# Second layer of the last two chunks by seven block products: decay attention and softplus FFN on one Trainium2 core

## The chip, the cores and the metric

The kernel runs on one core of one Trainium2 chip. Times are device microseconds of one execution. An execution's own time is a little longer than the span between its first and last instruction, and both are given where it matters. Engines are named as in the profile: PE (matmul) and PEld (its weight loads), DVE (vector), ACT (scalar), POOL (GpSimd), SP (the engine that issues most DMAs).

## The reference

```python
for b in range(nb):                       # nb = 12 blocks of 64 tokens
    qb, kb, vb = (q[:, :, sl], k[:, :, sl], v[:, :, sl])
    intra = einsum(qb, kb) * Dmask        # Dmask[i, j] = lam ** (i - j) for i >= j, else 0
    out[:, :, sl] = intra @ vb + (qb * lam_pow) @ kv_state
    kv_state = lam ** 64 * kv_state + (kb * rev_pow).T @ vb
x = out.transpose(0, 2, 1, 3).reshape(B * S, H * D)       # (3072, 512)
h = x @ w_in                                              # w_in (512, 2048)
g = maximum(h, 0) + log1p(exp(-abs(h)))                   # softplus
y = g @ w_out                                             # w_out (2048, 512)
```

All arrays are float32; q, k, v are (4, 8, 768, 64): batch 4, 8 heads, 768 tokens, 64 features.

## The kernel before

The sequence is cut into six chunks of 128 tokens (`NCH = 6`); a chunk holds these tokens of all four batches, 512 columns. Per chunk there is the attention (pairs of heads, `NP = 4`, called units), then two layers. To keep float32 accuracy at the fast matmul type, each operand is held as a high and a low part, and each product is three matmuls: high by high, high by low, low by high. d_ff = 2048 is cut into `NF = 16` blocks f of 128.

- Chunks 0 and 1 (`STD = 2`) run both layers plainly: `mlp1` (L421) and `mlp2` (L442). In this stretch the weights are also converted, the attention of later units is run, and the weights' parts go to DRAM scratch: `g1`, `g2` (blocks of w_in with the sums of blocks that the seven products need, made by `block_sums` and `store_sums`, L518 to L532) and `g3` (w_out).
- Chunks 2 and 3, and chunks 4 and 5, are taken in pairs. Their first layer uses seven products of blocks in place of eight (Winograd's form of Strassen): a product is one pair of f blocks i, a pair of halves of d_model, a pair of chunks. `product` (L588) does one, six matmuls. In the loop over c = 2, 4 and i = 0 to 7 the order on PE is P1 (bank a), P6 (bank b), P5 (bank c), P2 (adds into a), P7 (into b), P4 (into b), P3 (into c). ACT copies P1 out of a to `p1` (L757) before P2 may add into a; DVE makes `u2` (L759) before P7 may add into b. What comes out is softplus of h for f blocks 2i and 2i+1 of chunk c, split into `ga` and `gb`, and of chunk c+1, kept in `lb`.
- The second layer is plain: `second` (L607), three matmuls for one f block and one batch b, accumulating over f in four banks. For chunk c its steps are put between the products of the next iteration (`rest`, run in shares of 2, 4 and 2); for chunk c+1 they follow as a block after the loop, with operands split as they go. `finish` copies a bank and sends the output.
- In the loop for c = 2 one attention unit per iteration is run as well: `k_decay` (ACT, L289) and `q_decay` (DVE, L296) at its start, `event` near its end. At its end stands `low_of(gb, c21)` (DVE, L599). At i = 1 of c = 2 the last block sums of w_in are made: `block_sums(7)`, `store_sums(7)`, `send_sums(7)`.

The order is written out by hand: every engine runs its instructions in program order, and waits where an operand or a buffer is not ready. Buffers come from pools by size: 21 of 8 KB a partition (`t8`), 7 of 4 KB (`t4`), 5 of 2 KB (`t2`); a load on SP waits until one is free. PSUM has four banks for outputs (`obank`), two for `bank`, and a double one for `work`.

Of the kernel before, what the change touches and what calls it, by code (L numbers as in the profile page):

```python
# [32 lines left out]
def decay_attention_softplus_ffn(  # L33
# [12 lines left out]
    dr = ctx.enter_context(tc.tile_pool(name="dr", bufs=1, space=bass.MemoryType.DRAM))  # L46
# [383 lines left out]
    def mlp2(ss):  # L430
        c = ss[0] // NF
        ends = ss[-1] % NF == NF - 1
        if ss[0] % NF == 0:
            o_tiles[c] = [obank(f"o{c}_{b}") for b in range(B)]
        if ends:
            ob = t8([128, B, 512], F32, f"ob{c}")
        for b in range(B):
            for s in ss:
                f = s % NF
                g, w = g_tiles[s], w_second(s)  # L440
                for n, (i, j) in enumerate(((0, 0), (0, 1), (1, 0))):
                    nc.tensor.matmul(  # L442
                        o_tiles[c][b], lhsT=g[:, i, b * 128 : (b + 1) * 128], rhs=w[:, j],
                        start=f == 0 and n == 0, stop=f == NF - 1 and n == 2,
                    )
            if ends:
                copy = nc.vector.tensor_copy if b % 2 else nc.scalar.copy
                copy(out=ob[:, b], in_=o_tiles[c][b])
                queue = nc.scalar if c == NCH - 1 and b % 2 == 0 else nc.sync
                queue.dma_start(out=out[b * S + c * C : b * S + (c + 1) * C, :], in_=ob[:, b])  # L450

    def w_group(j):
        return (2 * j, 2 * j + 1) if 2 * j < NW else ()
# [90 lines left out]
    def load_w1(i):  # L544
        a, b = t8([128, 2, 4, 256], F32R, f"w1a{i}"), t8([128, 2, 3, 256], F32R, f"w1b{i}")
        nc.sync.dma_start(out=a.bitcast(F32), in_=g1[i])
        nc.sync.dma_start(out=b.bitcast(F32), in_=g2[i])
        w1_tiles[i] = a, b
# [49 lines left out]
    def low_of(g, l):  # L598
        nc.vector.tensor_sub(out=g[:, 1], in0=l, in1=g[:, 0])  # L599
# [12 lines left out]
    def finish(c, b):  # L612
        if c not in obs:
            obs[c] = t8([128, B, 512], F32, f"ob{c}")
        end = c == NCH - 1 and b % 2
        copy = nc.vector.tensor_copy if end else nc.scalar.copy
        copy(out=obs[c][:, b], in_=outs[c, b])
        queue = nc.sync if end else nc.scalar
        queue.dma_start(out=out[b * S + c * C : b * S + (c + 1) * C, :], in_=obs[c][:, b])

    def seconds(c, fs, ends=False):

# [105 lines left out]
    run(old_seconds([last - 4, last - 3]))  # L728
    rest = old_seconds([last - 2, last - 1], True)
    nxt = 4 * NP + 1  # L730
    for c in range(STD, NCH, 2):
        more = c + 2 < NCH
        lb = {}
        gs = {}
        for i in range(NF // 2):
            if more and i == 1:
                block_sums(NF // 2 - 1)
                store_sums(NF // 2 - 1)
                send_sums(NF // 2 - 1)
            unit = nxt if more else None  # L740
            if unit is not None:
                load_upto(unit + 2)
            if i + 1 < NF // 2:
                load_w1(i + 1)
            load_w2(i)
            if unit is not None and unit < NG:
                k_decay(unit)
                q_decay(unit)
            if i % 2 == 0:
                l4 = t8([128, 4, 512], F32, f"lb{c}_{i}")  # L750
            for n in range(2):
                lb[2 * i + n] = l4[:, 2 * (i % 2) + n]
            ta, tb = t4([128, 2, 512], F32, f"ta{c}_{i}"), t4([128, 2, 512], F32, f"tb{c}_{i}")
            p1, u2, u3, c21 = ta[:, 0], ta[:, 1], tb[:, 0], tb[:, 1]
            a, b_ = bank(f"a{c}_{i}"), work(f"b{c}_{i}")[:, 0]
            product("P1", i, a)
            nc.scalar.copy(out=p1, in_=a)  # L757
# [12 lines left out]
            low_of(ga, la)  # L770
            run(rest, 2)
            product("P4", i, b_, False)
            nc.vector.tensor_add(out=c21, in0=b_, in1=p1)
            nc.scalar.activation(c21, c21, AF.Softplus)
            gb = parts_of(f"g{c}_{2 * i + 1}", c21)
            product("P3", i, c_, False)
            nc.vector.tensor_add(out=u2, in0=c_, in1=u2)
            nc.scalar.activation(lb[2 * i], u2, AF.Softplus)
            run(rest, 4)
            if unit is not None and unit <= NG:  # L780
                event(unit)
                nxt += 1
            low_of(gb, c21)
            run(rest)
            pair = [(2 * i + n, (ga, gb)[n], w2_tiles[i][:, n]) for n in range(2)]
            rest = seconds(c, pair, i == NF // 2 - 1)
        ahead = 2
        def split(f):
            gs[f] = parts_of(f"g{c + 1}_{f}", lb[f])
            low_of(gs[f], lb[f])  # L790
        for f in range(ahead):
            split(f)
        for i in range(2):
            load_w2(i)
        run(rest)
        xc.clear()
        steps = []
        if more:
            steps = [lambda n=n, m=m: x_block(n, xr[c + 2][:, m + (2 if n == "P2" else 0)], m) for n in ("P1", "P2") for m in range(2)]
            for n in range(2):  # L800
                steps += [lambda n=n: x_sums_early(c + 2, n), lambda n=n: x_sums_late(c + 2, n)]
        for f in range(NF - 2):
            if f % 2 == 0 and f // 2 + 2 < NF // 2:
                load_w2(f // 2 + 2)
            if f + ahead < NF:
# [7 lines left out]
    run(rest)  # L813


def _layout(q, k, v, lam, w_in, w_out):
# [37 lines left out]
```

## Time and profile before

| | |
|---|---|
| time, median of 3 runs | 597.03 us (596.62 to 598.16) |
| profiled execution: time, span | 595.9 us, 594.1 us |
| PE busy | 576.5 us, 97% of the span |
| DVE busy | 321.6 us, 54% |
| ACT busy | 256.8 us, 43% |
| HBM read, written | 112.20 MB, 29.36 MB |
| granted PE clock | 0.999 of full speed |

The profile gives busy time and idle time by engine, by line and by stretch of time; a wait is put down to the instruction that ended it. An average over the span hides that the stretches differ: the first 226 us hold the attention, the conversion of weights and the plain chunks, the rest the two pairs of chunks. A row of a timeline reads: start, duration, engine, line, operation, output and inputs, shapes, how many were merged, and in square brackets the idle time before it with what ended it.

### The profile page before, as it was taken

To read this page: it belongs to the slowest core of one execution; us is meant where nothing else is said; L and a number is where in the kernel's file an instruction comes from. 1 tells how busy PE (TensorE), PEld (TensorE's weight loads), DVE (VectorE), ACT (ScalarE), POOL (GpSimd) and SP (SyncE) were. 2 spreads that over 40 slices of the span, in tenths; PEclk is the share of its full clock that TensorE was granted. 3 is DMA by queue.
4 is the path that set the end of the run, shared out by engine and by line. 5 is a ranking of instruction groups with operands and counts; after the bars stand their busy time and mean duration, and the time that the engine had idled before them with its cause. 6 is when DMAs were issued, how large, how long until landed. Compare 5 with 4: busy or idle time off the path is not lost.

```text
span 594.1 us, 12014 instructions
## 1 busy us (share of the span) xinstructions
PE 576.5 (97%) x5203; PEld 469.4 (79%) x5203; DVE 321.6 (54%) x492; ACT 256.8 (43%) x416; POOL 4.1 (1%) x11
## 2 busy tenths in 40 slices
PE   8899989989999999989999999999999999999997
PEld 6677778768888888778888888888888888888886
DVE  7779998974767768664543443295133333333410
ACT  3777776663345434543333332463142222224310
POOL 2000000000000000000000000000000000000000
PEclk9999999999999999999999999999999999999999
DMA  8997565883999974649965647489267454473101
GB/s 292 407 407 272 186 202 178 273 298 114 327 399 387 412 285 172 253 159 386 413 257 188 237 171 271 155 315 375 88 237 294 167 190 140 137 288 121 56 1 71
DMA packets 38452, 142.34 MB, mean 240 GB/s; under 512 B 3712, under 2 KB 5760, under 8 KB 31360
## 3 DMA queue, kind: packets, MB, share of 16 engines
q1 hardware_dynamic: 35808, 136.86, 62.7%
q10 hardware_dynamic: 2592, 4.72, 2.1%
q8 instruction: 41, 0.67, 0.5%
q14 instruction: 11, 0.09, 0.0%
HBM read 112.20 MB, written 29.36 MB: 238 GB/s over the span
## 4 chain that ended last, share of the span: by engine, by line
PE 76%; DVE 10%; DMA 8%; ACT 2%; issue 1%; SPq 1%; DVEq 0%; ACTq 0%
PE o L607 30%; PE b L588 11%; PE h L421 8%; PE o L442 8%; PE c L588 7%; PE a L588 7%; DMA att<-in_att 4%; DMA g<-w 3%; PE x L311 2%; PE z L326 2%; DVE c L235 2%; DVE st L343 2%; DMA raw<-in_wts 1%; DVE w L242 1%; DVE c L229 1%
## 5 line engine op out<-in xcount | busy, mean ns | idle before, releaser
L607 PE MATMUL o<-w,g 128*128 128x512 f32 x816 | 192.7, 390 | 0.0
L607 PEld LDWEIGHTS o<-w,g 128*128 128x128 f32 x816 | 152.5, 188 | 31.9
L421 PE MATMUL h<-x,w 128*128 128x512 f32 x384 | 94.4, 395 | 2.1 <-DVE w L242 2.1
L421 PEld LDWEIGHTS h<-x,w 128*128 128x128 f32 x384 | 70.9, 188 | 19.9 <-DVE w L242 3.7
L442 PE MATMUL o<-w,g 128*128 128x512 f32 x336 | 82.3, 393 | 1.1 <-DVE w L242 0.8
L442 PEld LDWEIGHTS o<-w,g 128*128 128x128 f32 x336 | 62.3, 188 | 15.1 <-DVE w L242 1.2
L588 PE MATMUL a<-xcP,w1a 128*128 128x512 f32 x192 | 49.0, 391 | 1.5 <-ACT ta L757 1.5
L588 PE MATMUL b<-xcP,w1b 128*128 128x512 f32 x192 | 48.8, 389 | 0.0
L759 DVE TENSOR_TENSOR ta<-b,ta 128x512 f32<-128x512 f32 x16 | 11.0, 690 | 60.9 <-PE b L588 60.9
L588 PEld LDWEIGHTS a<-xcP,w1a 128*128 128x128 f32 x192 | 35.9, 188 | 9.8 <-ACT ta L757 2.3
L588 PEld LDWEIGHTS b<-xcP,w1b 128*128 128x128 f32 x192 | 36.0, 188 | 7.5
L402 ACT ACTIVATE l<-h 128x512 f32<-128x512 f32 x32 | 19.0, 595 | 49.1 <-PE h L421 46.5
L599 DVE TENSOR_TENSOR g<-lb,g 128x512 fp32r<-128x512 f32 x32 | 21.1, 688 | 34.1 <-ACT g L595 34.1
L767 DVE TENSOR_TENSOR tb<-b,ta 128x512 f32<-128x512 f32 x16 | 11.1, 691 | 50.4 <-PE b L588 50.4
L338 DVE TENSOR_TENSOR a<-x,mask 128x512 f32<-128x512 f32 x15 | 10.4, 691 | 44.1 <-PE y L313 23.4
L410 DVE TENSOR_TENSOR g<-l,g 128x512 fp32r<-128x512 f32 x32 | 22.1, 690 | 18.8 <-ACT g L406 18.7
L764 ACT ACTIVATE la<-a 128x512 f32<-128x512 f32 x16 | 9.6, 598 | 52.3 <-PE a L588 52.3
L757 ACT COPY ta<-a 128x512 f32<-128x512 f32 x16 | 9.3, 584 | 51.8 <-PE a L588 51.8
L595 ACT CAST g<-lb 128x512 fp32r<-128x512 f32 x32 | 18.7, 619 | 18.4 <-PE o L607 17.6
L588 PE MATMUL b<-xcP,w1a 128*128 128x512 f32 x96 | 24.9, 391 | 0.8 <-DVE xcP L561 0.4
L326 PEld LDWEIGHTS z<-qd,st 64*64 64x64 f32 x640 | 17.0, 134 | 10.0 <-issue 9.7
L386 ACT COPY xr<-z 128x512 f32<-128x512 f32 x16 | 9.4, 585 | 36.0 <-PE z L330 35.5
(100 smaller groups left out, 774.4 us busy)
## 6 DMA issues: line engine op xcount, KB each, us to landing
w<-g SPq DMA_DIRECT2D x39, 1024.0 KB, 5.6
att<-in_att SPq DMA_DIRECT2D x48, 512.0 KB, 10.0
raw<-in_wts SPq DMA_DIRECT2D x32, 512.0 KB, 10.2
w1a<-g SPq DMA_DIRECT2D x16, 1024.0 KB, 6.8
g<-w SPq DMA_DIRECT2D x24, 512.0 KB, 9.3
w1b<-g SPq DMA_DIRECT2D x16, 768.0 KB, 6.7
g<-parts SPq DMA_DIRECT2D x16, 512.0 KB, 9.0
out_dram<-ob ACTq DMA_DIRECT2D x18, 256.0 KB, 2.0
```

The source lines that it names most:

```text
L235: nc.vector.tensor_add(out=c, in0=c, in1=raw_at(ks, 0))
L311: nc.tensor.matmul(x[r, cols], lhsT=k[r, b, t], rhs=q[r, b, t], start=True, stop=True)
L326: nc.tensor.matmul(w[half(t), s, cols], lhsT=st[r, b, t], rhs=qd[r, b, t], start=True, stop=False)
L343: nc.vector.scalar_tensor_tensor(out=to[:, :, t], in0=of[:, :, t], scalar=lam_c[r, h : h + 1], in1=u[:, :, t], op0=ALU.mult, op1=ALU.add,)
L402: nc.scalar.activation(l_tiles[s], h_tiles.pop(s), AF.Softplus)
L410: nc.vector.tensor_sub(out=g[:, 1, :], in0=l_tiles.pop(s), in1=g[:, 0, :])
L421: nc.tensor.matmul(h_tiles[s], lhsT=w[:, i, cs], rhs=x[:, j, :], start=p == 0 and n == 0, stop=p == NP - 1 and n == 2,)
L442: nc.tensor.matmul(o_tiles[c][b], lhsT=g[:, i, b * 128 : (b + 1) * 128], rhs=w[:, j], start=f == 0 and n == 0, stop=f == NF - 1 and n == 2,)
L588: nc.tensor.matmul(to, lhsT=w[:, k, n, p * 128 : (p + 1) * 128], rhs=x[:, j, p], start=start and p == 0 and m == 0, stop=p == 1 and m == 2 ...
L595: nc.scalar.copy(out=g[:, 0], in_=l)
L599: nc.vector.tensor_sub(out=g[:, 1], in0=l, in1=g[:, 0])
L607: nc.tensor.matmul(outs[c, b], lhsT=g[:, i, b * 128 : (b + 1) * 128], rhs=w[:, j], start=f == 0 and n == 0, stop=f == NF - 1 and n == 2,)
```

## The change

The second layer of the last pair (chunks 4 and 5) is done by seven block products too, transposed: the result has d_model on partitions and the chunk's columns along the bank. A product now runs over all eight pairs of f blocks, one product after another (P1, P6, P2, P7, P5, P4, P3), with the two halves of 128 output rows in two banks. The sums of w_out blocks that this needs are made in the loop for c = 2 (`out_block_sums`, `out_block_low`) from the w2 tile that is loaded there anyway, and are written to a DRAM scratch (`v_sums`) by `send_out_sums`; they are loaded again product by product (`load_v`). The first layer of the last pair gets a loop of its own, without second-layer steps between its products; its P4 and P3 are put off into the next iteration, and its softplus results stay in eight `act` tiles. The operands of a product are made and split five products ahead (`split_upto`). The last two chunks go to a second output, `out_t`, transposed, and are put in their rows when the two outputs are joined.

```diff
@@ mlp2, finish: the last chunk's outputs are no longer shared between two queues
-                queue = nc.scalar if c == NCH - 1 and b % 2 == 0 else nc.sync
-                queue.dma_start(out=out[...], in_=ob[:, b])
+                nc.sync.dma_start(out=out[...], in_=ob[:, b])
@@
+    def out_block_sums(i):
+        w = w2_tiles[i]
+        box = t8([128, 4, DM], F32, f"full2_{i}")
+        full, s1, s2, s3, s4 = ...
+        nc.vector.tensor_add(out=full, in0=w[:, :, 0], in1=w[:, :, 1])
+        nc.vector.tensor_add(out=s1, in0=a21, in1=a22)
+        nc.vector.tensor_sub(out=s3, in0=a11, in1=a21)
+        nc.vector.tensor_sub(out=s2, in0=s1, in1=a11)
+        nc.vector.tensor_sub(out=s4, in0=a12, in1=s2)
+        parts = t8([128, 2, 4, 256], F32R, f"parts2_{i}")
+        nc.scalar.copy(out=parts[:, 0]..., in_=box[:, 2:4]...)
+        out_parts[i] = box, parts
+
+    def out_block_low(i):
+        nc.vector.tensor_sub(out=parts[:, 1]..., in0=box[:, 2:4]..., in1=parts[:, 0]...)
+
+    def send_out_sums(i):
+        for n, p in enumerate(("P5", "P6", "P7", "P3")):
+            nc.sync.dma_start(out=v_sums[p][:, i], in_=parts[:, :, n])
@@ the loop over pairs, now for c = 2 alone
-    for c in range(STD, NCH, 2):
+    for c in range(STD, NCH - 2, 2):
@@ end of an iteration i
             low_of(gb, c21)
+            if i >= 2:
+                send_out_sums(i - 2)
+            if i >= 1:
+                out_block_low(i - 1)
+            out_block_sums(i)
             run(rest)
@@ before and in the second layer of chunk 3
+        out_block_low(NF // 2 - 1)
+        send_out_sums(NF // 2 - 2)
         for f in range(NF - 2):
+            if f == 2:
+                send_out_sums(NF // 2 - 1)
@@ first layer of the last pair
+    for i in range(NF // 2):
+        ...
+        product("P1", i, a)
+        nc.scalar.copy(out=p1, in_=a)
+        product("P6", i, b_)
+        nc.vector.tensor_add(out=u2, in0=b_, in1=p1)
+        run(late)                       # P4 and P3 of the iteration before
+        ...
+        product("P5", i, c_)
+        product("P2", i, a, False)
+        nc.scalar.activation(b11, a, AF.Softplus)
+        product("P7", i, b_, False)
+        ...
+        if i >= 2:
+            second_parts(i - 2)         # two subtractions and additions on DVE
+            split_upto(i - 1)
@@ second layer of the last pair
+    for j, p in enumerate(order):
+        ...
+        if j + 2 < len(order):
+            load_v(order[j + 2])
+        for i in range(NF // 2):
+            ...
+            split_upto(8 * j + i + 6)
+            for n in range(2):
+                out_product(p, i, n)    # three matmuls, lhsT = v tile, rhs = split operand
+        ...
+            for n in range(2):
+                take(p, n)              # a bank read by ACT or DVE, sent when complete
```

More of the change, by code (lines that the diff above doesn't have):

```diff
@@ L39, in decay_attention_softplus_ffn @@
     out: bass.AP,
+    out_t: bass.AP,
 ):
@@ L448, in mlp2 @@
                 copy(out=ob[:, b], in_=o_tiles[c][b])
-                queue = nc.scalar if c == NCH - 1 and b % 2 == 0 else nc.sync
-                queue.dma_start(out=out[b * S + c * C : b * S + (c + 1) * C, :], in_=ob[:, b])
+                nc.sync.dma_start(out=out[b * S + c * C : b * S + (c + 1) * C, :], in_=ob[:, b])
     def w_group(j):
@@ L535, in decay_attention_softplus_ffn @@
     ready = {}
+    v_sums = {p: dr.tile([128, NF // 2, 2, 256], F32, name=f"v{p}", tag=f"v{p}") for p in ("P5", "P6", "P7", "P3")}
+    out_parts = {}
+    def out_block_sums(i):
+        w = w2_tiles[i]
+        box = t8([128, 4, DM], F32, f"full2_{i}")
+        full, s1, s2, s3, s4 = box[:, 0:2], *[box[:, 2 + n // 2, n % 2 * 256 : n % 2 * 256 + 256] for n in range(4)]
+        nc.vector.tensor_add(out=full, in0=w[:, :, 0], in1=w[:, :, 1])
+        a11, a21 = full[:, 0, 0:256], full[:, 0, 256:512]
+        a12, a22 = full[:, 1, 0:256], full[:, 1, 256:512]
+        nc.vector.tensor_add(out=s1, in0=a21, in1=a22)
[3 more added lines that the diff above has]
+        parts = t8([128, 2, 4, 256], F32R, f"parts2_{i}")
+        nc.scalar.copy(out=parts[:, 0].rearrange("q n c -> q (n c)"), in_=box[:, 2:4].rearrange("q n c -> q (n c)"))
+        out_parts[i] = box, parts
+    def out_block_low(i):
+        box, parts = out_parts[i]
+        nc.vector.tensor_sub(
+            out=parts[:, 1].rearrange("q n c -> q (n c)"), in0=box[:, 2:4].rearrange("q n c -> q (n c)"),
+            in1=parts[:, 0].rearrange("q n c -> q (n c)"),
+        )
+    def send_out_sums(i):
+        parts = out_parts.pop(i)[1].bitcast(F32)
+        for n, p in enumerate(("P5", "P6", "P7", "P3")):
+            nc.sync.dma_start(out=v_sums[p][:, i], in_=parts[:, :, n])
     def send_sums(i):
@@ L614, in finish @@
             obs[c] = t8([128, B, 512], F32, f"ob{c}")
[L615 to L619, printed above, removed]
+        nc.scalar.copy(out=obs[c][:, b], in_=outs[c, b])
+        nc.scalar.dma_start(out=out[b * S + c * C : b * S + (c + 1) * C, :], in_=obs[c][:, b])
     def seconds(c, fs, ends=False):
@@ L730, in decay_attention_softplus_ffn @@
     nxt = 4 * NP + 1
-    for c in range(STD, NCH, 2):
-        more = c + 2 < NCH
+    for c in range(STD, NCH - 2, 2):
+        more = True
         lb = {}
@@ L812, in decay_attention_softplus_ffn, with second_parts, split_hi @@
         rest = seconds(c + 1, [(f, gs[f], w2_tiles[f // 2][:, f % 2]) for f in (NF - 2, NF - 1)], True)
-    run(rest)
+    c = NCH - 2
+    act = {}
+    def second_parts(i):
+        b11, b12, b22 = act[i][:, 0], act[i][:, 1], act[i][:, 3]
+        nc.vector.tensor_sub(out=b12, in0=b22, in1=b12)
+        nc.vector.tensor_add(out=b12, in0=b12, in1=b11)
+    splits = {}
+    order = ("P1", "P6", "P2", "P7", "P5", "P4", "P3")
+    todo = [(p, i) for p in order for i in range(NF // 2)]
+    def split_hi(p, i):
+        b11, t2_, b21, b22 = [act[i][:, n] for n in range(4)]
+        plain = {"P1": b11, "P6": t2_, "P2": b21, "P3": b22}
+        if p in plain:
+            of = plain[p]
+        else:
+            of = t2([128, 512], F32, f"t{p}_{i}")
+            a, b = {"P7": (t2_, b11), "P5": (b22, t2_), "P4": (b21, t2_)}[p]
+            nc.vector.tensor_sub(out=of, in0=a, in1=b)
+        g = splits[p, i] = t4([128, 2, 512], F32R, f"s{p}_{i}")
+        nc.scalar.copy(out=g[:, 0], in_=of)
+        return g, of
@@ new lines, in decay_attention_softplus_ffn, with split_upto, load_v @@
+    n_split, waiting = 0, []
+    def split_upto(n):
+        nonlocal n_split
+        while n_split < min(n, len(todo)):
+            waiting.append(split_hi(*todo[n_split]))
+            n_split += 1
+            if len(waiting) > 1:
+                low_of(*waiting.pop(0))
+        if n >= len(todo):
+            while waiting:
+                low_of(*waiting.pop(0))
+    vt = {}
+    def load_v(p):
+        for m in range(2):
+            t = vt[p, m] = t8([128, 4, 2, 256], F32R, f"v{p}_{m}")
+            if p in v_sums:
+                nc.sync.dma_start(out=t.bitcast(F32), in_=v_sums[p][:, 4 * m : 4 * m + 4])
+            else:
+                odd, side = {"P1": (0, 0), "P2": (1, 0), "P4": (1, 1)}[p]
+                for k in range(4):
+                    nc.sync.dma_start(
+                        out=t[:, k].bitcast(F32), in_=g3[4 * m + k][:, odd, :, side * 256 : side * 256 + 256]
+                    )
@@ new lines, in decay_attention_softplus_ffn, with late_21, late_12 @@
+    late = []
+    for i in range(NF // 2):
+        if i + 1 < NF // 2:
+            load_w1(i + 1)
+        else:
+            load_v(order[0])
+        act[i] = t8([128, 4, 512], F32, f"act{i}")
+        b11, b12, b21, b22 = [act[i][:, n] for n in range(4)]
+        ta = t4([128, 2, 512], F32, f"ta{c}_{i}")
+        p1, u2 = ta[:, 0], ta[:, 1]
+        first = i == 0
+        a = bank(f"a{c}_{i}") if first else obank(f"a{c}_{i}")
+        b_ = work(f"b{c}_{i}")[:, 0] if first else obank(f"b{c}_{i}")
+        product("P1", i, a)
[3 more added lines that the diff above has]
+        run(late)
+        if first:
+            run(rest, 5)
+        c_ = bank(f"c{c}_{i}")
+        product("P5", i, c_)
+        product("P2", i, a, False)
+        nc.scalar.activation(b11, a, AF.Softplus)
+        if first:
+            run(rest, 4)
+        product("P7", i, b_, False)
+        nc.vector.tensor_add(out=b22, in0=b_, in1=p1)
+        nc.vector.tensor_add(out=b22, in0=c_, in1=b22)
+        nc.scalar.activation(b22, b22, AF.Softplus)
+        if first:
+            run(rest)
+        def late_21(i=i, b_=b_, p1=p1, b21=b21):
+            product("P4", i, b_, False)
+            nc.vector.tensor_add(out=b21, in0=b_, in1=p1)
+            nc.scalar.activation(b21, b21, AF.Softplus)
+        def late_12(i=i, c_=c_, u2=u2, b12=b12):
+            product("P3", i, c_, False)
+            nc.vector.tensor_add(out=b12, in0=c_, in1=u2)
+            nc.scalar.activation(b12, b12, AF.Softplus)
+        late = [late_21, late_12]
+        if i >= 2:
+            second_parts(i - 2)
+            split_upto(i - 1)
@@ new lines, in decay_attention_softplus_ffn, with send, take @@
+    run(late)
+    xc.clear()
+    load_v(order[1])
+    split_upto(6)
+    second_parts(NF // 2 - 2)
+    split_upto(7)
+    second_parts(NF // 2 - 1)
+    post = [t8([128, 4, 512], F32, f"post{n}") for n in range(2)]
+    c11 = t8([128, 2, 512], F32, "c11")
+    banks = {}
+    def send(of, cc, side, n):
+        row = side * 256 + n * 128
+        queue = nc.sync if n else nc.scalar
+        queue.dma_start(out=out_t[cc, row : row + 128], in_=of)
+    def take(p, n):
+        p1, u2, u3, c21 = [post[n][:, m] for m in range(4)]
+        if p == "P1":
+            nc.scalar.copy(out=p1, in_=banks["a", n])
+        elif p == "P6":
+            nc.vector.tensor_add(out=u2, in0=banks["b", n], in1=p1)
+        elif p == "P2":
+            nc.scalar.copy(out=c11[:, n], in_=banks["a", n])
+            send(c11[:, n], 0, 0, n)
+        elif p == "P7":
+            nc.vector.tensor_add(out=u3, in0=banks["b", n], in1=p1)
+        elif p == "P5":
+            nc.vector.tensor_add(out=u3, in0=banks["c", n], in1=u3)
+            send(u3, 1, 1, n)
+        elif p == "P4":
+            nc.vector.tensor_add(out=c21, in0=banks["b", n], in1=p1)
+            send(c21, 0, 1, n)
+        else:
+            nc.vector.tensor_add(out=u2, in0=banks["c", n], in1=u2)
+            send(u2, 1, 0, n)
@@ new lines, in out_product @@
+    def out_product(p, i, n):
+        g, w, k = splits[p, i], vt[p, i // 4], i % 4
+        fresh = p in ("P1", "P6", "P5")
+        to = banks[{"P1": "a", "P2": "a", "P5": "c", "P3": "c"}.get(p, "b"), n]
+        for m, (x, y) in enumerate(((0, 0), (0, 1), (1, 0))):
+            nc.tensor.matmul(
+                to, lhsT=w[:, k, x, n * 128 : n * 128 + 128], rhs=g[:, y],
+                start=fresh and i == 0 and m == 0, stop=i == NF // 2 - 1 and m == 2, skip_group_check=True,
+            )
@@ new lines, in decay_attention_softplus_ffn @@
+    for j, p in enumerate(order):
+        if p in ("P1", "P6"):
+            for n in range(2):
+                banks["a" if p == "P1" else "b", n] = obank(f"r{p}_{n}")
+        if p == "P5":
+            for n in range(2):
+                banks["c", n] = bank(f"r{p}_{n}")
+        if j + 2 < len(order):
+            load_v(order[j + 2])
+        for i in range(NF // 2):
+            if p == order[-1] and i >= NF // 2 - 4:
+                break
+            split_upto(8 * j + i + 6)
+            for n in range(2):
+                out_product(p, i, n)
+        if p == order[-1]:
+            split_upto(len(todo))
+            for n in range(2):
+                for i in range(NF // 2 - 4, NF // 2):
+                    out_product(p, i, n)
+                take(p, n)
+        else:
+            for n in range(2):
+                take(p, n)
@@ L849 @@
     o = nc.dram_tensor("out_dram", (B * S, DM), F32, kind="ExternalOutput").ap()
+    ot = nc.dram_tensor("out_t_dram", (2, DM, B * C), F32, kind="ExternalOutput").ap()
     with tile.TileContext(nc) as tc:
-        decay_attention_softplus_ffn(tc, *args, o)
+        decay_attention_softplus_ffn(tc, *args, o, ot)
     r = run_bass_kernel_spmd(nc, [feed], core_ids=[0])
-    return r.results[0]["out_dram"]
+    y = np.array(r.results[0]["out_dram"]).reshape(B, NCH, C, DM)
+    yt = np.asarray(r.results[0]["out_t_dram"]).reshape(2, DM, B, C)
+    y[:, NCH - 2 :] = yt.transpose(2, 0, 3, 1)
+    return y.reshape(B * S, DM)
```

## Prediction

> **What bounds the kernel now.** I read the page first (engines, chain, costliest groups), then the stages by windows, then the chain in order of time, then the timelines of PE, DVE and ACT where the change adds work.
>
> From the page: TensorE, the chain by engine, and the second layer's matmuls.
>
> ```profile
> PE 576.5 (97%) x5203; PEld 469.4 (79%) x5203; DVE 321.6 (54%) x492; ACT 256.8 (43%) x416; POOL 4.1 (1%) x11
> ...
> PE 76%; DVE 10%; DMA 8%; ACT 2%; issue 1%; SPq 1%; DVEq 0%; ACTq 0%
> ...
> L607 PE MATMUL o<-w,g 128*128 128x512 f32 x816 | 192.7, 390 | 0.0
> ```
>
> The stages (us; PE, PEld, DVE, ACT, POOL busy; granted clock, DMA share, GB/s): first layer of the pair of chunks 2 and 3 with the second layer of chunk 2 (to 376.70), second layer of chunk 3, first layer of chunks 4 and 5 with the second layer of chunk 4 (to 541.50), second layer of chunk 5, tail.
>
> ```profile
> 262.40:376.70 114.30, 114.25 (x1207) 94.56 (x1207) 47.91 (x77) 40.35 (x70) 0.00 (x0) 1.00 0.73 272
> 376.70:421.80 45.10, 45.10 (x203) 37.35 (x200) 23.32 (x38) 19.49 (x35) 0.00 (x0) 1.00 0.74 280
> 421.80:541.50 119.70, 119.70 (x530) 99.12 (x529) 39.20 (x58) 37.87 (x62) 0.00 (x0) 1.00 0.51 185
> 541.50:590.50 49.00, 48.99 (x217) 40.22 (x215) 9.93 (x15) 11.74 (x20) 0.00 (x0) 1.00 0.17 54
> 590.50:594.10 3.60, 0.00 (x0) 0.00 (x0) 0.69 (x1) 0.00 (x0) 0.00 (x0) 0.83 0.39 146
> ```
>
> From 262.40 to 590.50 PE is full: it is the bound, and both a matmul saved and a wait added show in the time one to one. The chain says what a matmul costs there:
>
> ```profile
> 421.85 1.36 PE a L588 x6
> ...
> 436.81 1.36 PE a L588 x6
> ...
> 537.45 53.05 PE o L607 x234
> ```
>
> 53.05/234 = 0.2267 us each, 1.36 us per group of six; an iteration i of the last pair is 14.96 us = 66 matmuls.
>
> **The saving.** The second layer of chunks 4 and 5 has 2 chunks x 16 f x 4 b x 3 = 384 matmuls now; by seven products, 7 x 8 pairs of f x 2 halves x 3 = 336. 48 x 0.2267 = **10.9 us off**, all of it on PE's path, if PE stays full.
>
> **The cost: out_block_sums in the loop of chunk 2.** Its instructions are put at the end of each iteration i, after low_of(gb): on DVE out_block_low(i-1) (1024 wide), a 1024-wide add and four 256-wide sums; on ACT a 1024-wide cast that waits for those sums. Both engines run in program order, so behind that cast stand the next iteration's k_decay (two kd) and its copy of P1 out of bank a; P2 accumulates into bank a and waits for that copy, and PE waits in order with it. Before has this very sequence once, at i=1, where block_sums(7) and store_sums(7) stand in the same place. PE, then DVE, then ACT there:
>
> ```profile
> 256.70 1.52 PE L588 MATMUL a<-xcP,w1a 128*128 128x512 f32 x6
> 259.42 1.52 PE L588 MATMUL c<-xcP,w1a 128*128 128x512 f32 x6
> 262.45 1.65 PE L588 MATMUL a<-xcP,w1a 128*128 128x512 f32 x6 [1.51 <-ACT ta L757]
> ```
>
> ```profile
> 256.48 0.69 DVE L599 TENSOR_TENSOR g<-tb,g 128x512 fp32r<-128x512 f32 x1
> 257.09 1.29 DVE L518 TENSOR_TENSOR full<-w 128x512 f32<-128x512 f32 x2
> 258.48 0.43 DVE L523 TENSOR_TENSOR sums<-full 128x256 f32<-128x256 f32 x1
> ...
> 259.61 0.43 DVE L526 TENSOR_TENSOR sums<-full,sums 128x256 f32<-128x256 f32 x1
> 261.15 1.23 DVE L532 TENSOR_TENSOR parts<-sums,parts 128x1024 fp32r<-128x1024 f32 x1 [1.12 <-ACT parts L531]
> 262.30 0.69 DVE L296 TENSOR_TENSOR qd<-att,lp 128x512 f32<-128x512 f32 x1
> ```
>
> ```profile
> 260.07 1.05 ACT L531 CAST parts<-sums 128x1024 fp32r<-128x1024 f32 x1 [2.58 <-DVE sums L526]
> 261.03 0.90 ACT L289 ACTIVATE kd<-att,rp 128x256 f32<-128x256 f32 x2
> 261.83 0.56 ACT L757 COPY ta<-a 128x512 f32<-128x512 f32 x1
> ```
>
> The sums end at 260.04, the cast starts 0.03 later, kd 0.96 after it, the copy 0.80 after that, and PE goes on 0.62 after the copy's start. PE began the iteration at 256.70 and P2 could have started three groups later, 4.08; it started 5.75 later.
>
> Elsewhere in this loop ACT is early and nothing of the kind is seen. Where low_of(gb) starts against the iteration's first matmul gives the room, for i=2, i=4 and i=7 (PE rows, then DVE rows):
>
> ```profile
> 275.73 1.52 PE L588 MATMUL a<-xcP,w1a 128*128 128x512 f32 x6
> ...
> 310.19 0.62 PE L588 MATMUL a<-xcP,w1a 128*128 128x512 f32 x2
> ...
> 361.88 0.62 PE L588 MATMUL a<-xcP,w1a 128*128 128x512 f32 x2
> ```
>
> ```profile
> 276.90 0.69 DVE L599 TENSOR_TENSOR g<-tb,g 128x512 fp32r<-128x512 f32 x1
> 277.51 0.68 DVE L296 TENSOR_TENSOR qd<-att,lp 128x512 f32<-128x512 f32 x1
> ...
> 310.45 0.69 DVE L599 TENSOR_TENSOR g<-tb,g 128x512 fp32r<-128x512 f32 x1
> ...
> 362.14 0.69 DVE L599 TENSOR_TENSOR g<-tb,g 128x512 fp32r<-128x512 f32 x1
> ```
>
> It starts 1.17 after P1 at i=2 (and at i=3, as there too four state updates go before it), and 0.26 at i=4 to 7 (the last chunk has two). From its start to P2's: 0.61 to the next DVE instruction (276.90 to 277.51), 1.15 for out_block_low (261.15 to 262.30), 1.25 for the 1024-wide add (1.23 of L532 and the wait for its result), 1.56 for the four sums (258.48 to 260.04), then 0.03 + 0.96 + 0.80 + 0.62: **6.98**. P2 is due at 4.08. So PE stands still at
> - i=2 and 3: 1.17 + 6.98 - 4.08 = 4.07 each, 8.14;
> - i=4, 5, 6: 0.26 + 6.98 - 4.08 = 3.16 each, 9.48;
> - i=7: 3.16 less the 0.80 of kd, which is no more there (no unit is left): 2.36;
> - i=1: the first add and sums (1.25 + 1.56, of which 0.07 runs into the next) go ahead of block_sums(7): 2.74 more than now.
>
> Sum **22.7 us on**. Nothing late comes in its place: P7 waits for u2 on DVE, which now follows the same copy by 0.7 and is done before P2 ends 1.36 later. Behind the waiting cast on ACT are only kd and the copies.
>
> **What I cost at nothing, and its cover.**
> - The last sums (i=7) delay ACT's casts for chunk 3 by the same chain, but PE has the 24 matmuls of the last pair (5.44 us) before it needs them. Cover gone: up to 2.4.
> - 8 MB of sums written to DRAM by SP in that loop: 272 GB/s at a share of 0.73 becomes some 342 at 0.92. Hidden while the share is under 1. The sends wait on SP for out_block_low of the iteration before, loads queue behind them.
> - out_block_sums(i) reads w2 tile i at 1.17 + 0.61 + 1.15 = 2.9 after the next P1, some 4 us before its first matmul (behind P7, at 6.8). Tile 1 is the closest: issued at 266.88, landed 10.9 later, at 277.8. The 2.74 of i=1 moves everything there; the add would start at 275.73 + 2.74 + 2.9 = 281.4, the landing be at 280.5. 0, with 0.9 to spare.
>
> ```profile
> 266.88 0.40 SPq L552 DMA_DIRECT2D w<-g  x1
> ...
> DMA to landing us min/median/max: 10.9/10.9/10.9
> ```
>
> - First layer of the last pair without second-layer matmuls between: 42 matmuls, 9.52 us. Per iteration DVE has 5 adds, 2 second_parts and a low part, ACT five evacuations and a cast: 8 x 0.69 = 5.5 and, at the 1.05 of a cast twice as wide, at most 6.3. P4 and P3 are put off into the next iteration, so each bank is read 2.7 us or more before it is due. 0.
> - The products: 336 matmuls in 76.2 us. The tightest are P7, P5, P4: 24 products, 32.6 us of PE; DVE 48 instructions for operands and six that take banks, 54 x 0.60 = 32.4 at its pace when nothing waits (three in 1.89, less 0.69, over two), 37.3 at the whole 0.69. The operands are issued five products (6.8 us) ahead, which covers the 4.7 between. 0; upper end 3.
>
> ```profile
> 240.78 1.89 DVE L561 TENSOR_TENSOR xcP<-tt,xcP 128x512 fp32r<-128x512 f32 x3
> ```
>
> - load_v: 14 MB in about 88 us, 160 GB/s, where 280 are moved at 376.70:421.80; each 2 MB is asked for 12 us or more ahead. P1, P2, P4 come in pieces of 1 KB, for which I have no load row. 0; upper end 2.
> - The tail: one DVE instruction and a 256 KB DMA after the last matmul as now, 3.6. Dropping the two-queue split in finish and mlp2 touches nothing that still runs at the end. 0.
>
> **Sum:** -10.9 + 22.7 = +11.8. The profiled execution took 595.9 (span 594.1), so it would be 607.7; the median shown, 597.03, is 1.1 above it, which gives **608.8**.
>
> **The rivals.**
> - *The clock falls in the new gaps.* PE idles 0.16 less than its start shifts (1.51 against 1.67 at i=1): gaps of 4.2, 3.9, 3.9, then three of 3.0 and one of 2.2. The longest gap after the start now is 2.94 and left the clock at 1.00; in the 3.60 after the last matmul it fell (0.83 above). Getting it back is seen at the start, where 18 matmuls took 6.39 for 4.24 at the full pace: 2.15 lost. Three gaps above what is known to be harmless: up to 6.5, **615.3**.
>
> ```profile
> 129.81 0.34 PE L326 MATMUL z<-qd,st 64*64 64x64 f32 x8 [2.94 <-DVE st L343]
> ...
> 126.80:129.90 3.10, 0.15 (x6) 0.12 (x9) 3.00 (x7) 1.04 (x1) 0.00 (x0) 1.00 1.01 316
> ...
> 1.45 6.39 PE L150 MATMUL warm_ps<-warm 128*128 128x512 f32 x18 [1.45 <-DVE warm L145]
> ```
>
> The Trainium skill, page "TensorE: Matmul & The Clock Gate", Part 1 with "HAM oscillation", speaks against the change here: idle gaps over some 3.4 us bring the clock to half, by a free-running window, so not each gap does. By that rule it is the three gaps named that are in danger; by the trace alone, which has no gap between 2.94 and 3.60, the sum would stand. The 2.94 row agrees with the rule; nothing here shows it at 3.9.
>
> - *Buffers run short.* The loop's loads already wait for one of 21 buffers; box and parts take three more. Landing times by the page, then the seventh w1a load and the sixth w2 load of this stretch:
>
> ```profile
> w<-g SPq DMA_DIRECT2D x39, 1024.0 KB, 5.6
> ...
> w1a<-g SPq DMA_DIRECT2D x16, 1024.0 KB, 6.8
> ...
> 315.83 0.33 SPq L546 DMA_DIRECT2D w1a<-g  x1
> ...
> 326.25 0.32 SPq L552 DMA_DIRECT2D w<-g  x1
> ```
>
> An iteration is (361.88 - 310.19)/3 = 17.23, so i=6 starts at 344.65. One iteration later, w1a would still have 11.6 before its use there, for a landing of 6.8; w2, needed at 344.65 + 2.9, would have 4.1 for 5.6: 1.5 late, four times, +6, **614.8**. For it: the waits on SP; against: longer iterations give the loads 3 us more each.
> - *ACT does not hold P1's copy up* (the other side: faster). Were the cast to let the copy pass, only DVE's order would count: u2 ends 1.17 + 0.61 + 1.15 + 1.25 + 1.56 + 0.6 + 0.7 = 7.0 after P1 where P7 is due at 5.44: 1.6 twice, 0.7 three times, and some 2.5 at i=1 for the 2.74 there, together 7.8: **593.9**. It decides once the chain from low_of(gb) to P2 is shorter than 2.9 (i=2) or 3.8 (i=4); the three ACT rows above, in program order, speak against.
> - *Everything is hidden*, DVE being 42% busy in that loop (47.91 of 114.30): **586.1**. Against: the work stands in one lump at the one place where PE needs the engine next.
>
> **Chances:** the sum as it stands 0.51, clock 0.22, buffers 0.09, DVE alone 0.07, all hidden 0.08, between these and no change 0.03. A measurement tells 0.3% (1.8 us) from nothing. Faster 0.16, same 0.02, slower 0.82. The likeliest case alone: 604 to 613 (the zeros' upper ends; stalls a tenth shorter). Range for 8 in 10, to the clock and buffer cases and leaving out the two fast ones: 599 to 617.
>
> **What would show it.** PE busy falls by about 11 and its idle time grows by 22 to 23. In the loop of chunk 2, iterations of some 20 to 21 us in place of 17.2, with PE idle before P2 of "a", released by ACT ta, three to four us each; in ACT's timeline the cast of the sums, kd and ta in a row. The last pair: 422 to 590 now, 157.8 us of nearly gapless PE after. Wrong if P2 starts on time there (then 586 to 594), or if PE waits in the last pair for g operands or v tiles.

## The result, and the profile after

The changed kernel takes 621.06 us (median of 4 runs, 619.28 to 624.14) against 596.83 (595.34 to 598.16): a ratio of 1.041, 95% interval 1.0386 to 1.0434. The forecast was slower, at 608.8 with a range to 617; it is slower by twice as much. The profiled execution took 619.28 with a span of 617.3, 23.2 more than before's 594.1.

From the page after: TensorE, its granted clock in 40 slices, the first matmul group that has idle time before it, and the new cast on ACT.

```profile
PE 577.6 (94%) x5155; PEld 467.0 (76%) x5155; DVE 395.4 (64%) x612; ACT 276.0 (45%) x446; POOL 4.1 (1%) x11
...
PEclk9999999999999999988977989999999999999999
...
L620 PE MATMUL a<-xcP,w1a 128*128 128x512 f32 x192 | 55.5, 429 | 23.2 <-ACT ta L786 23.2
...
L554 ACT CAST parts<-full 128x1024 fp32r<-128x1024 f32 x8 | 8.4, 1046 | 44.0 <-DVE full L552 31.8
```

PE has 48 matmuls fewer, yet is busy 1.1 us longer, and the mean matmul into bank a went from 391 to 429 ns. The second line says why: in slices 18 to 24, the loop of chunk 2, the clock was not the full one. The third has the waits: 23.2 us ahead of "a", ended by ACT's copy of P1; before it was 1.5.

The stages after (us; PE, PEld, DVE, ACT, POOL busy; clock, DMA share, GB/s), divided where PE's timeline goes from one to the next: loop of chunk 2 from the wait at i = 1 on, second layer of chunk 3, first layer of the last pair, its second layer, tail.

```profile
262.00:409.71 147.71, 126.00 (x1206) 101.39 (x1207) 74.51 (x118) 48.03 (x80) 0.00 (x0) 0.92 0.64 229
409.71:454.73 45.02, 45.02 (x205) 37.28 (x199) 25.98 (x43) 20.44 (x36) 0.00 (x0) 1.00 0.94 356
454.73:537.43 82.70, 81.92 (x362) 67.51 (x360) 36.95 (x56) 27.94 (x48) 0.00 (x0) 1.00 0.56 191
537.43:613.70 76.27, 76.27 (x337) 62.88 (x335) 55.61 (x90) 33.57 (x56) 0.00 (x0) 1.00 0.34 130
613.70:617.30 3.60, 0.05 (x1) 0.00 (x0) 0.69 (x1) 0.00 (x0) 0.00 (x0) 0.86 0.20 73
```

The same stages in the profile before; here both layers of the last pair are one row:

```profile
262.00:376.67 114.67, 114.22 (x1207) 94.53 (x1207) 48.31 (x78) 40.74 (x71) 0.00 (x0) 1.00 0.73 271
376.67:421.69 45.02, 45.02 (x205) 37.27 (x200) 23.32 (x38) 19.49 (x35) 0.00 (x0) 1.00 0.74 280
421.69:590.50 168.81, 168.80 (x745) 139.46 (x743) 49.13 (x73) 49.61 (x82) 0.00 (x0) 1.00 0.41 147
```

The loop is 33.0 us longer: all of the loss stands there. The last pair is as good as full, as before, has 48 matmuls less and is 9.8 us shorter. One iteration of the loop (i = 2) in the timelines of PE, DVE and ACT:

```profile
279.55 1.52 PE L620 MATMUL a<-xcP,w1a 128*128 128x512 f32 x6
...
282.27 1.52 PE L620 MATMUL c<-xcP,w1a 128*128 128x512 f32 x6
287.69 1.79 PE L620 MATMUL a<-xcP,w1a 128*128 128x512 f32 x5 [3.89 <-ACT ta L786]
```

```profile
280.72 0.69 DVE L631 TENSOR_TENSOR g<-tb,g 128x512 fp32r<-128x512 f32 x1
281.33 1.22 DVE L559 TENSOR_TENSOR parts<-full,parts 128x1024 fp32r<-128x1024 f32 x1
282.47 1.22 DVE L546 TENSOR_TENSOR full<-w 128x1024 f32<-128x1024 f32 x1
283.72 0.42 DVE L549 TENSOR_TENSOR full<-full 128x256 f32<-128x256 f32 x1
...
284.85 0.42 DVE L552 TENSOR_TENSOR full<-full 128x256 f32<-128x256 f32 x1
```

```profile
285.31 1.04 ACT L554 CAST parts<-full 128x1024 fp32r<-128x1024 f32 x1 [6.95 <-DVE full L552]
286.26 0.90 ACT L290 ACTIVATE kd<-att,rp 128x256 f32<-128x256 f32 x2
287.07 0.56 ACT L786 COPY ta<-a 128x512 f32<-128x512 f32 x1
```

P1 is complete at 281, and its copy starts at 287.07, because ACT had been standing before the cast for 6.95 us. PE stands for 3.89.

What follows on the gaps is in the same trace by windows of 3.41 us (columns as above; PE busy is the first, the clock the third from the end):

```profile
124.75:128.16 3.41, 1.62 (x8) 0.99 (x6) 3.24 (x5) 2.27 (x4) 0.00 (x0) 1.00 0.96 327
...
285.17:288.59 3.42, 0.90 (x4) 0.76 (x5) 1.40 (x3) 2.32 (x4) 0.00 (x0) 1.00 1.03 430
288.59:292.00 3.41, 3.41 (x10) 2.63 (x9) 0.00 (x0) 1.22 (x2) 0.00 (x0) 0.50 0.96 343
305.65:309.07 3.42, 1.22 (x6) 0.68 (x4) 3.17 (x6) 0.74 (x1) 0.00 (x0) 1.00 1.02 353
309.07:312.48 3.41, 1.78 (x4) 1.49 (x5) 0.69 (x1) 1.58 (x4) 0.00 (x0) 0.50 0.95 325
312.48:315.89 3.41, 3.41 (x9) 2.63 (x8) 0.00 (x0) 1.21 (x2) 0.00 (x0) 0.50 0.46 162
...
329.55:332.96 3.41, 1.13 (x5) 0.59 (x4) 2.19 (x6) 1.72 (x3) 0.00 (x0) 1.00 0.92 327
332.96:336.37 3.41, 2.75 (x7) 2.20 (x8) 0.69 (x1) 0.60 (x2) 0.00 (x0) 0.50 0.99 372
...
377.33:380.74 3.41, 1.69 (x7) 1.43 (x8) 0.69 (x1) 1.67 (x4) 0.00 (x0) 1.00 1.00 418
380.74:384.15 3.41, 3.41 (x16) 2.81 (x15) 1.98 (x3) 1.22 (x2) 0.00 (x0) 1.00 0.70 209
```

The clock is at half through whole windows: 3.41 us from 264.69, 288.59 and 356.85, 6.83 from 309.07 and 332.96, 23.9 us in all. Ten matmuls stand in the full window from 288.59, sixteen in the one from 380.74. PE was busy for 21.4 of the 23.9, and in the window from 288.59 a matmul starts every 0.427 in place of every 0.227: by these numbers about 10.0 us are lost, an estimate.

### The profile page after: what moved, and what is told of

Read it like the earlier page. It is cut to its first block, busy times and chain, and to the rows that moved or that the text cites. A ratio compares the mean times of both kernels' runs of the same rounds, so it can differ in the third digit from the quotient of the medians.

```text
span 617.3 us, 12182 instructions
## 1 busy us (share of the span) xinstructions
PE 577.6 (94%) x5155; PEld 467.0 (76%) x5155; DVE 395.4 (64%) x612; ACT 276.0 (45%) x446; POOL 4.1 (1%) x11
## 4 chain that ended last, share of the span: by engine, by line
PE 71%; DVE 15%; ACT 5%; DMA 4%; issue 4%; SPq 1%; ACTq 0%; DVEq 0%
PE o L639 13%; PE rP L995 12%; PE h L422 9%; PE b L620 9%; PE o L443 8%; PE a L620 6%; PE c L620 5%; PE z L327 2%; PE x L312 2%; DVE st L344 2%; DMA w<-g 2%; PE z L331 2%; DVE w L243 2%; DVE c L236 1%; DMA raw<-in_wts 1%
## 5 line engine op out<-in xcount | busy, mean ns | idle before, releaser
L639 PE MATMUL o<-w,g 128*128 128x512 f32 x432 | 104.1, 393 | 0.0
L639 PEld LDWEIGHTS o<-w,g 128*128 128x128 f32 x432 | 81.2, 189 | 17.4
L443 PE MATMUL o<-w,g 128*128 128x512 f32 x336 | 82.5, 394 | 1.1 <-DVE w L243 0.8
L620 PE MATMUL a<-xcP,w1a 128*128 128x512 f32 x192 | 55.5, 429 | 23.2 <-ACT ta L786 23.2
L995 PE MATMUL rP<-sP,vP 128*128 128x512 f32 x336 | 76.3, 389 | 0.0
L443 PEld LDWEIGHTS o<-w,g 128*128 128x128 f32 x336 | 62.3, 188 | 15.3 <-DVE w L243 1.4
L995 PEld LDWEIGHTS rP<-sP,vP 128*128 128x128 f32 x336 | 63.1, 188 | 13.1
L620 PE MATMUL b<-xcP,w1b 128*128 128x512 f32 x192 | 53.0, 415 | 0.8 <-DVE act L932 0.8
L554 ACT CAST parts<-full 128x1024 fp32r<-128x1024 f32 x8 | 8.4, 1046 | 44.0 <-DVE full L552 31.8
L932 DVE TENSOR_TENSOR act<-b,ta 128x512 f32<-128x512 f32 x8 | 5.5, 692 | 31.1 <-PE b L620 31.1
L631 DVE TENSOR_TENSOR sP<-act,sP 128x512 fp32r<-128x512 f32 x32 | 20.9, 686 | 6.5 <-ACT sP L875 6.5
L875 ACT CAST sP<-act 128x512 fp32r<-128x512 f32 x32 | 19.2, 619 | 13.0 <-PE rP L995 6.8
```

The costliest lines, as they stand in the source:

```text
L443: nc.tensor.matmul(o_tiles[c][b], lhsT=g[:, i, b * 128 : (b + 1) * 128], rhs=w[:, j], start=f == 0 and n == 0, stop=f == NF - 1 and n == 2,)
L620: nc.tensor.matmul(to, lhsT=w[:, k, n, p * 128 : (p + 1) * 128], rhs=x[:, j, p], start=start and p == 0 and m == 0, stop=p == 1 and m == 2 ...
L639: nc.tensor.matmul(outs[c, b], lhsT=g[:, i, b * 128 : (b + 1) * 128], rhs=w[:, j], start=f == 0 and n == 0, stop=f == NF - 1 and n == 2,)
L875: nc.scalar.copy(out=g[:, 0], in_=of)
L995: nc.tensor.matmul(to, lhsT=w[:, k, x, n * 128 : n * 128 + 128], rhs=g[:, y], start=fresh and i == 0 and m == 0, stop=i == NF // 2 - 1 and ...
```

## The experiments

Two theories could explain the distance between 608.8 and 621. **Theory C:** the waits are as forecast, and the clock that falls behind them costs the rest. **The rival, B:** the loop is short of buffers or DMA. Beside them stood the question whether the order on ACT (**theory A**) is really the cause of the waits.

### The cast alone moved (e1_cast_later)

```diff
@@ out_block_sums(i): the cast becomes a function of its own, out_block_high(i)
@@ loop of chunk 2
             product("P1", i, a)
             nc.scalar.copy(out=p1, in_=a)
+            if i >= 1:
+                out_block_high(i - 1)
             product("P6", i, b_)
@@ behind the loop, ahead of out_block_low(NF // 2 - 1): out_block_high(NF // 2 - 1)
```

> The cast of the w_out sums on ACT stands one step later: behind the copy of P1 in the next iteration, where ACT is idle; the DVE work stays where it was. Theory A (ACT's program order: the cast holds the copy of P1, which holds P2): PE's waits before P2 go away at i=2 to 7, what is left is P7 waiting for u2 behind DVE's lump, some 1.5 us at i=2 and 3, 0.7 at i=4 to 6, and the 4.3 us gap at i=1, where the cast of the w_in sums still stands in front. Waits 7.8 us instead of 22.6 and at most one fall of the clock: 592 to 596. Rival B (the loop is short of buffers or of DMA, and the waits only show up at P2): the time stays within 3 us of 621.

604.11 us (601.71 to 604.94), ratio to before 1.0112 (1.0082 to 1.0143). The waits ahead of P2 went, except at i=1, and P7's wait for u2 stands at 1.38, 1.32, 0.58 and 0.58, as theory A has it. The time missed the expectation by 8 us. PE's and ACT's timelines of this kernel:

```profile
289.04 0.72 PE L624 MATMUL b<-xcP,w1b 128*128 128x512 f32 x2 [1.38 <-DVE ta L794]
...
357.06 0.49 PE L327 MATMUL z<-qd,st 64*64 64x64 f32 x8 [4.39 <-DVE tb L808]
```

```profile
353.49 1.04 ACT L558 CAST parts<-full 128x1024 fp32r<-128x1024 f32 x1 [13.34 <-DMA vP<-parts]
```

The cast at i=5 waited 13.34 us, released by a DMA that sent older sums away: it had no buffer to write to. Behind it stood the softplus of bank a and all else on ACT, and PE lost 4.39. The clock then stayed at half from 355.88 to 362.71, with PE busy for 5.65 of it: about 2.6 us more, estimated as above. Most of the 8 us is in these two. This is the buffer rival, at a place where the changed kernel itself does not show it.

### The sends first on SP (e8_send_first)

```diff
@@ e1_cast_later, start of iteration i
+            if i >= 2:
+                send_out_sums(i - 2)
             unit = nxt if more else None
@@ end of iteration i
-            if i >= 2:
-                send_out_sums(i - 2)
```

> The kernel with the cast moved behind the copy of P1, and on SP the sends of the sums of tile i-2 at the start of iteration i, ahead of that iteration's loads, in place of its end. Theory (buffers: there the cast of tile 4 waited 13.3 us for a buffer that the sends of tile 2 held, which queued on SP behind loads that waited for buffers themselves; PE lost 4.4 us and, through the clock, 2.8 more): the gap at i=5 goes away, 604.1 becomes 596 to 599. Rival (the buffer is short whatever the order): within 2 us of 604.

598.80 us (596.26 to 599.23), ratio 1.003 (1.0009 to 1.0052). The 4.39 gap is gone, the u2 waits are the same. On ACT the same cast still waits for its buffer, but 4.92 in place of 13.34, and PE no longer feels it:

```profile
344.48 1.05 ACT L558 CAST parts<-full 128x1024 fp32r<-128x1024 f32 x1 [4.92 <-DMA vP<-parts]
```

So the buffer was short mainly through the order on SP: the sends that free it stood behind loads that waited for buffers themselves.

### Everything moved to where DVE waits (e2_mid)

```diff
@@ loop of chunk 2, cast of tile i-2 behind the copy of P1, then
             nc.scalar.activation(lb[2 * i], u2, AF.Softplus)
+            if i >= 2:
+                out_block_low(i - 2)
+            if i >= 1:
+                out_block_sums(i - 1)
             run(rest, 4)
@@ end of iteration i: only send_out_sums(i - 2) is left
@@ what is left of the last two tiles goes into the second layer of chunk 3 (f = 1 and f = 3)
```

> Also the DVE part is moved: out_block_sums of tile i-1 and out_block_low of tile i-2 go ahead of the event in the middle of iteration i, where DVE waited 4.07 us for the scores; the cast goes behind the next copy of P1. Same instructions, same count. Theory A: the loop of chunk 2 is back to 17.2 us an iteration, with only the old 1.5 us gap at i=1, and the 48 matmuls saved show: 596.8 - 10.9 + 0.8 (P4 at the end of the first layer) = 586 to 588. Rival B (buffers or DMA): some of the 24 us stay, 600 or more. Rival D (the seven-product block itself is slower than 336 matmuls back to back): above 590 with gaps after 400 us.

587.71 us (586.82 to 588.94), ratio 0.9852 (0.983 to 0.9875): faster than before, with the same instructions as the changed kernel. From its page, then its DVE and ACT timelines:

```profile
PE 566.0 (97%) x5155; PEld 459.9 (79%) x5155; DVE 395.2 (68%) x612; ACT 276.4 (47%) x446; POOL 4.1 (1%) x11
...
L624 PE MATMUL a<-xcP,w1a 128*128 128x512 f32 x192 | 49.0, 390 | 1.5 <-ACT ta L790 1.5
```

```profile
287.00 1.22 DVE L563 TENSOR_TENSOR parts<-full,parts 128x1024 fp32r<-128x1024 f32 x1
288.14 1.22 DVE L546 TENSOR_TENSOR full<-w 128x1024 f32<-128x1024 f32 x1
...
290.52 0.43 DVE L552 TENSOR_TENSOR full<-full 128x256 f32<-128x256 f32 x1
291.16 0.69 DVE L339 TENSOR_TENSOR a<-x,mask 128x512 f32<-128x512 f32 x1 [0.21 <-PE y L314]
```

```profile
294.11 0.59 ACT L790 COPY ta<-a 128x512 f32<-128x512 f32 x1 [1.96 <-PE a L624]
294.59 1.05 ACT L558 CAST parts<-full 128x1024 fp32r<-128x1024 f32 x1
```

In the kernel before, DVE waits for the scores of the event in the same place:

```profile
291.57 0.69 DVE L338 TENSOR_TENSOR a<-x,mask 128x512 f32<-128x512 f32 x1 [4.07 <-PE y L313]
```

These 4.07 us now hold 3.95 of sums, and 0.21 is left; the copy of P1 is again released by PE, and the cast follows it into idle time. The wait ahead of bank a is the old 1.5. With e1_cast_later, where the cast alone took away the waits ahead of P2, this shows theory A: the order on ACT and DVE makes all of the new waits in this loop. PE has no other wait in the loop, so neither DMA nor a buffer holds it up here (DMA has a share of 0.75 from 262.05 to 380.00). Two small gaps of PE come after the loop: 0.78 at the last P4, told below, and 0.62 at 384.00, released by a copy of chunk 2's outputs on ACT, which the changed kernel does not have.

### The sums without the saving (e4_sums_only)

```diff
@@ the kernel before, end of an iteration i of the loop of chunk 2
             low_of(gb, c21)
+            if more:
+                if i >= 2:
+                    send_out_sums(i - 2)
+                if i >= 1:
+                    out_block_low(i - 1)
+                out_block_sums(i)
```

> The kernel before with the sums of w_out blocks made and written to the DRAM scratch in the loop of chunk 2, as the change does, and never read; the second layer of the last pair stays plain. Theory A and C: the waits (22.5) and the half clock (about 10, it depends on where the gaps fall) without the saving: 596.8 + 33 = 627 to 633. Rival (part of the 24 us is lost in the last pair): below 622.

632.93 us (626.62 to 633.48), ratio 1.0585 (1.0532 to 1.0638), in the expected band: 11.9 more than the changed kernel, where the sum has 10.9 saved less 0.9 lost in the last pair. The spread is wide; in the profiled execution, which took 626.62, the clock fell in four windows of the loop.

### Filling the gaps (e3_fill10, e7_fill12)

```diff
@@ the changed kernel, e3_fill10: between P5 and P2, i >= 1
+            for _ in range(10):
+                nc.tensor.matmul(bw[:, 1], lhsT=..., rhs=..., start=True, stop=True)
@@ the changed kernel, e7_fill12: ahead of P5, into the bank that P5 clears
+            for _ in range(12):
+                nc.tensor.matmul(c_, lhsT=..., rhs=..., start=True, stop=True)
```

> The changed kernel with ten more matmuls (2.27 us) between P5 and P2 in the loop of chunk 2 for i of 1 and more; they go to an unused PSUM bank and nothing reads them. The copy of P1 that P2 waits for comes at the same time, so PE's total delay is the same, but no gap is above 2.1 us. Theory C (of the 24 us, 10.7 are matmuls at half clock after the gaps): granted clock 1.00, time 621.1 - 10.7 = 609 to 612, less than without these matmuls. Rival (half clock costs little, since it falls into waits; the rest is buffers): 619 to 623, or more by the matmuls added.

646.61 us (646.02 to 646.97), ratio 1.0837 (1.0818 to 1.0857): a miss, through the experiment itself. The PE timeline shows the added matmuls (L793) waiting, not filling:

```profile
294.20 1.22 PE L793 MATMUL b<-xcP,w1a 128*128 128x512 f32 x2 [4.61 <-DVE ta L789]
```

They went to the other half of the tile that bank b is part of, and were held until DVE had read b. The gaps grew by 0.7 to 1.2 each, ten matmuls came after every one, and the clock fell in all seven. It says nothing on theory C.

> The changed kernel with twelve more matmuls (2.72 us) ahead of P5 in the loop of chunk 2 for i of 1 and more, into the bank that P5 then clears, so nothing waits for them and nothing reads them. The run with ten into another bank did not fill the gaps, since its matmuls themselves waited for u2 on DVE (gaps of 3.0 to 5.5 before them): here they stand in front of the wait. P2 waits for the same copy of P1, so PE's delay is unchanged, but the gaps of 4.3, 3.9, 3.8, three of 3.0 and 2.3 become 1.6, 1.2, 1.1, three of 0.3 and none. Theory C (half clock after the gaps costs 10.7 of the 24 us): clock 1.00 and 609 to 612, some 10 less than the changed kernel in spite of 84 more matmuls. Rival (half clock costs little): 620 to 625.

611.13 us (609.49 to 611.91), ratio 1.024 (1.0222 to 1.0258): 9.9 less than the changed kernel, with 84 matmuls more. The clock line of its page and PE's timeline at i=2:

```profile
PEclk9999999999999999999999999999999999999999
```

```profile
286.27 1.65 PE L620 MATMUL a<-xcP,w1a 128*128 128x512 f32 x6 [1.18 <-ACT ta L786]
```

The waits for the copy are as long as they were, only filled (twelve matmuls of 0.227 and 1.18 make 3.90, for 3.89), and in the profiled execution the clock stays full; in the other three its mean is 0.993 to 0.997, as in executions of before. Theory C holds: half clock was worth some 10 us.

### The last sums of w_in moved too (e5_mid_w7)

```diff
@@ e2_mid: block_sums(7) and store_sums(7) from the start of i = 1 to the middle of i = 0
+            if i == 0:
+                block_sums(NF // 2 - 1)
+                store_sums(NF // 2 - 1)
```

> The kernel with the sums of w_out in the middle of the iterations, and the last sums of w_in (block_sums and store_sums of 7) moved the same way, from the start of i=1 to the middle of i=0. Theory A (a cast on ACT that waits for DVE ahead of the copy of P1 is what costs): the 1.5 us gap at i=1, which the kernel before has too, goes as well: 587.7 - 1.6 = 586. Rival (DVE has no room in i=0 beside the late x sums: the wait moves to u2 or the scores): 587 or more.

588.11 us (587.61 to 588.30), ratio 0.9848 (0.9834 to 0.9863). The gap went from 1.52 to 0.33:

```profile
262.99 0.50 PE L624 MATMUL a<-xcP,w1a 128*128 128x512 f32 x1 [0.33 <-ACT ta L788]
```

The time did not follow: it is no different from 587.71. In this profile the clock fell once near 129, at a gap that before has too, and in the profile of e2_mid it did not; 3.4 us at half clock cost some 1.6, the size of what was to be gained. That does not settle it, though: all four executions here have a mean clock of 0.997, and the one of e2_mid with that mean took 588.20. Whether this edit is worth anything stays open.

## Why the prediction was wrong, point by point

- **The saving** was right. PE has 48 matmuls fewer; the second layer's 336 run back to back, from 537.43 to 613.70.
- **The waits, place and size,** were right. The chain from low_of(gb) to P2 was put at 6.98 and is 287.69 - 280.72 = 6.97. Idle gaps were put at 4.2, 3.9, 3.9, three of 3.0 and 2.2; they are 4.27, 3.89, 3.83, 2.93, 2.98, 3.02 and 2.30.
- **The clock** is the step that failed. The sum held it at nothing, and the rival that had it got a chance of 0.22, a price of 2.15 a gap and three gaps. It fell behind five of the seven, and stayed down for a second window in two of them: 10 us by the fill experiment. The price of a gap was about right, 2.0 on the mean; the number of gaps was not. For the three gaps of 3.8 and more the prediction had no row that left the clock alone, and its sum still put them at nothing. For the others the error in the reading was to take one gap of 2.94 that left the clock alone as proof that a gap of this length is harmless. In other profiles here the clock fell at that very gap. Of the signs that the prediction named, PE's idle time grew as forecast (39.7 us for 17.6), but PE busy, which was to fall by 11, rose by 1.1: that difference is the clock.
- **When the clock fell.** What sorts the cases is not the gap's length but how much PE was busy in a fixed window: the rows above fell with 0.90, 1.22 and 1.13 us of work in 3.41 and held with 1.62 and 1.69. Over all profiles of this case, past the first 30 us, every window with 1.49 us or less was followed by half clock, and every one with 1.51 or more by the full clock. (The first 30 us do not follow this, see the last section.) A 3 us gap that falls mostly into one window leaves some 0.4 to 1.4 of work there, a gap split evenly over two leaves 1.9 in each. So at 3 us it is the phase that counts, which differs from execution to execution, and each such gap should have carried a part of the price in the main sum. The executions of the changed kernel differ in the same way: with a mean clock of 0.980 they took 619.28 and 620.35, with 0.974 and 0.972 they took 621.76 and 624.14.
- The Trainium skill, page "TensorE: Matmul & The Clock Gate", Part 1, describes a free-running window of 3413 ns. The trace agrees: the falls are 23.90, 20.48, 23.89 and 23.89 us apart, 7, 6, 7 and 7 windows, and each lasts one window or two. The Trainium skill's advice on the same page, section "Why this matters for your kernels", to leave no gaps over some 3 us is near, but behind a gap of 2.93 the clock fell, behind one of 3.02 it held, and windows that fell were not all idle ones; the measurement decides. The two gaps:

```profile
333.62 0.80 PE L620 MATMUL a<-xcP,w1a 128*128 128x512 f32 x1 [2.93 <-ACT ta L786]
...
379.05 0.50 PE L620 MATMUL a<-xcP,w1a 128*128 128x512 f32 x1 [3.02 <-ACT ta L786]
```

- **What was costed at nothing** held, but for one. The w2 tiles were there in time, the writes were hidden, the products' operands and v tiles made PE wait nowhere, the tail is 3.60 as before. The exception: at the end of the first layer PE waits 0.78, since the last P4 has no next iteration to be put off into and follows P7 at once, so that the 2.7 us claimed for every bank are 0 there:

```profile
534.55 1.66 PE L620 MATMUL b<-xcP,w1b 128*128 128x512 f32 x6 [0.78 <-DVE act L932]
```

- **The rivals.** Buffers: not in the changed kernel, but they decided the first experiment. DVE alone: what e1_cast_later and e8_send_first show at P7, 1.4 twice and 0.6 three times where 1.6 and 0.7 were worked out. All hidden: what e2_mid is, at 587.7 where 586.1 was worked out.

The account: -10.9 saved, +22.7 of waits (21.7 of idle time more than before, and for each of six new gaps the 0.16 by which a start shifts more than PE idles), +0.9 at the last P4, +10.0 of half clock make 22.7, for 23.2 more of span. 0.5 is not assigned.

## What to carry to other kernels

An instruction that waits for another engine costs what stands behind it on its own engine: before adding work to a loop, find which PSUM copy follows it in that engine's program order, and put the work behind that copy or into a stretch where the producer waits anyway. The same instructions were worth +24 us or -9 us by place alone. And where waits of 2 us or more on PE come regularly, price the clock with them: count the busy time that is left in a window of 3.4 us, not the length of the gap, and where the window falls is not known, give each gap a part of the price.

## What was not expected of the hardware

The clock of a kernel that keeps PE 97% busy still falls now and then: before has one gap of 2.94 us, ended by DVE at 129.81. In its profile the window around it kept 1.6 us of work and the clock held; in the profiles of e4_sums_only and e8_send_first, the same gap, unchanged, left 0.8 and 0.9 in a window and the clock fell. Before's executions with a mean clock of 1.000 took 595.42 and 595.77, those at 0.993 to 0.996 took 596.7 to 598.1. Much of the 0.5% between runs of one kernel thus goes with the clock.

A return to the full clock asks more than a hold does: after 309.07 a window with 1.78 us of work, and after 332.96 one with 2.75, were each followed by another at half clock, while 1.62 was enough to hold it at full. Over all profiles past the first 30 us, windows at half clock with 2.46 or less were followed by another and those with 2.84 or more by the full clock; two with 2.76 went one each way.

In the first 30 us, where attention with matmuls of 64x64 runs, busy time does not sort the windows. In e1_cast_later the clock fell behind one with 1.69 us of work, and two windows at half clock that PE filled were each followed by another:

```profile
7.72:11.13 3.41, 1.69 (x66) 1.50 (x65) 2.13 (x3) 1.62 (x3) 0.87 (x2) 1.00 1.02 418
11.13:14.55 3.42, 3.42 (x63) 2.26 (x65) 2.72 (x5) 1.90 (x5) 0.87 (x1) 0.50 1.03 412
14.55:17.96 3.41, 3.41 (x69) 2.25 (x62) 2.73 (x5) 2.15 (x4) 0.00 (x0) 0.50 1.03 405
```

In e8_send_first it fell behind one with 1.98. These windows hold 52 to 69 matmuls each, mostly small ones; that small matmuls count for less than their busy time would explain it, and is not shown.
